# The second transform of a Fourier and MLP kernel: its fold moved behind the length-49 product, its token split moved to GpSimd

## The chip, the cores and the metric

One core of a Trainium2 chip runs the whole kernel in one launch. The metric is device time in microseconds (us), a median over runs; lower is better. The engines named below are TensorE (PE in the rows; PEld is its weight load), VectorE (DVE), ScalarE (ACT), GpSimd (POOL) and SyncE (SP), which issues every DMA of this kernel on one queue.

## What is computed

Three blocks follow each other on x of shape 2 x 3136 x 256 (batch, tokens, channels), all float32:

```python
# 1: a filter in the frequency domain along the tokens
X = np.fft.rfft(x, axis=1)
Yr = Xr @ w_r - Xi @ w_i + b_r ; Yi = Xr @ w_i + Xi @ w_r + b_i    # then a soft threshold of 0.01
y = np.fft.irfft(Y, n=3136, axis=1)
# 2: x + relu(layernorm(x) @ w_ch1) @ w_ch2, with a gain, 256 -> 1024 -> 256
# 3: a Fourier mix and another MLP of that size
mixed = np.real(np.fft.fft(np.fft.fft(x, axis=1), axis=2))
u = x + mixed
out = u + relu(layernorm(u) @ w_ch1) @ w_ch2
```

The change lies in the Fourier mix of block 3. A transform of length 3136 is done as 49 x 64: a length-49 product over the tokens, then a length-64 one, and a length-256 one over the channels. Since only the real part is wanted and the channel transform is symmetric, channel c and channel 256 - c are first combined: a sum in channels 1 to 127 and a difference in channels 129 to 255. Channels 0 and 128 have no partner. The combination ("the fold") is linear and acts on channels, the length-49 product acts on tokens, so either can come first.

## The kernel before

The tokens lie as 98 rows (49 x 2) of 32 x 256 = 8192 columns. Blocks 1 to 3 are staged so that TensorE always has work: the MLP of block 2 (`mlp1`, 13 chunks of up to 512 tokens) and that of block 3 (`mlp2`, 13 chunks) are the two long runs, and other work is hung on them by *hooks*: a hook `(k, "l1", f)` runs a function behind hidden block f (0 to 7) of chunk k, a hook `(k, "l2", i)` behind output tile i (0 to 3). The hooks set the priority; a planner, which estimates the time of every instruction, then writes each engine's order, and an engine works strictly in that order.

*A chunk.* `l1(f)` (L630 on) is six matmuls into one of three PSUM tiles "a" (lines L220 to L222 inside `mm3r`), ScalarE's ReLU (L641) and VectorE's remainder of it (L642), which frees the tile. `l2(i)` is eight pairs of matmuls (L658, L659) into PSUM "b" and two VectorE adds (L662, L663). `prep` normalizes the next chunk: statistics and small arithmetic on VectorE (L586 to L595) and, for the chunks marked `by_act` (`mlp1[8:12]` and `mlp2[1:5]`), the application on ScalarE in two passes of up to four instructions (L602 with a bias, L603 with a scale). The bias of L602 is the negated mean, a 128 x 4 tile `ng` made by VectorE at L599. `trans` then transposes on TensorE (L617, PSUM "c") and rounds the result into two parts, on ScalarE (L622 or L202) and VectorE (L623 or L210).

*The second transform, first half.* `Stage98` (L330 on) works in 16 steps per batch, each on 98 x 512 raw tokens. `load` brings them by DMA (L348) into the ring `r98` of four tiles, which `Front.load` (L706, the same ring) shares for what `mlp2` reads. `split` folds on GpSimd (L360 sum, L361 difference, L362 the two channels without a partner), rounds the result to its high part on ScalarE (`a_copy`, L202 in the rows, tile `s`) and subtracts that on GpSimd for the low part (L210, tile `s`). `step` multiplies with three matmuls (L220 to L222 into PSUM "c"), copies the 98 x 512 result on ScalarE (L202, tile `o`), lays two columns of channel 128, which come from a small product of their own (`middle`, `middle2`), over it on GpSimd (L405) and stores it (L406). `start` loads the middle column, loads two tiles and splits both at once. The ring `t98` of two tiles serves the transposes of block 1 and, in `mlp1`, the decoding of block 3's weights (lines L509 to L517).

*Where it runs.* Batch 0 starts behind output tile 0 of chunk 7 of `mlp1`, with its first step at `(8, "l1", 0)` and five steps to a chunk in chunks 8 to 10. Batch 1 starts behind output tile 0 of chunk 0 of `mlp2`, with its first step at `(0, "l2", 2)` and five steps to a chunk in chunks 1 to 3. These chunks of `mlp2` also run `Front.dmix` in their first layer, VectorE work of some seven instructions per pair (L205, L754 to L759) that ends in additions of two SBUF tiles (L756, L759).

Of the kernel before, what the change touches and what calls it, by code (L numbers as in the profile page):

```python
# [9 lines left out]
F32 = mybir.dt.float32  # L10
# [6 lines left out]
R98, S98, O98 = 4, 8, 4  # L17
# [18 lines left out]
PREP_BEHIND = (3, 2, 0)  # L36
APPLY_POOL = (0, 1)
APPLY_CHUNKS = 2
STAGE4_AT = ((8, "l1", 0),) + tuple((k, *at) for k in (8, 9, 10) for at in
                                    (("l1", 2), ("l1", 5), ("l2", 0), ("l2", 1), ("l2", 3)))  # L40
STAGE4_MLP2 = ((0, "l2", 2),) + tuple((k, *at) for k in (1, 2, 3) for at in
                                      (("l1", 2), ("l1", 5), ("l2", 0), ("l2", 1), ("l2", 3)))
STAGE4_FROM = ((7, "l2", 0), (0, "l2", 0))
WARM_UP = 10
TB = 2
I64 = mybir.dt.int64
AF = mybir.ActivationFunctionType
ALU = mybir.AluOpType
# [5 lines left out]
D = 256  # L54
NQ = 98
# [107 lines left out]
def fourier_moe_kernel(ctx, tc, x, w_r, w_i, b_r, b_i, g_ln, w11, w12, w21, w22,  # L163
                       t_ca, t_cam, t_cim, t_cb, t_ci, t_cb0, t_ci0, t_cd, t_ident, out):
    nc = tc.nc
# [3 lines left out]
    wk = ctx.enter_context(tc.tile_pool(name="wk", bufs=2))  # L169
# [5 lines left out]
    def psum(tag):  # L175
        return pp.tile([128, 512], F32, tag="ps" + tag, name="ps" + tag, bufs=ps_bufs[tag])
# [4 lines left out]
    def qslot(dt=F32R):  # L181
        return wk.tile([128, 1024], dt, tag="q", name="q", bufs=3)

    def wslot(dt=F32, n=128):
        return wk.tile([n, 512], dt, tag="w", name="w", bufs=WB)
# [15 lines left out]
    def a_copy(o, i, scale=1.0):  # L201
        nc.scalar.activation(out=o, in_=i, func=AF.Copy, scale=scale)  # L202
# [6 lines left out]
    def sub(eng, o, a, b):  # L209
        ins = eng.tensor_tensor(out=o, in0=a, in1=b, op=ALU.subtract)  # L210
        mark["pool" if eng is nc.gpsimd else "dve"] = getattr(ins, "ins", ins)
# [6 lines left out]
    def mm3r(ps, lh, ll, rh, rl, first, last):  # L218

        nc.tensor.matmul(out=ps, lhsT=lh, rhs=rh, start=first, stop=False)  # L220
        nc.tensor.matmul(out=ps, lhsT=ll, rhs=rh, start=False, stop=False)  # L221
        ins = nc.tensor.matmul(out=ps, lhsT=lh, rhs=rl, start=False, stop=last)  # L222
        mark["pe"] = getattr(ins, "ins", ins)
# [54 lines left out]
    class Forward:  # L278
# [7 lines left out]
        def load(self, k, cut=1):  # L286
            t = self.slot()[0:NQ]
            w = 1024 // cut
            for e in range(cut):
                ins = sp.dma_start(out=t[:, e * w:(e + 1) * w],  # L290
                                   in_=x[self.b, k][:, e * w:(e + 1) * w])
                mark["sp"] = getattr(ins, "ins", ins)
            self.raw[k] = t

        def step(self):
            g = self.g
            if g >= 16:
                return
            e = g % 2
            ps = psum(self.tag)  # L300
            nc.tensor.matmul(out=ps, lhsT=cam, rhs=self.raw[g // 2][:, e * 512:(e + 1) * 512], start=True, stop=True)  # L301
            ins = nc.vector.transpose(out=yg[self.b].rearrange("p k c -> p c k")[:, g * 16:(g + 1) * 16, :],
                                      in_=ps.rearrange("p (c j) -> p c j", j=32))
            mark["dve"] = getattr(ins, "ins", ins)
            self.g += 1
# [24 lines left out]
    def s98():  # L330
        return [next(s98_ring)[0:NQ] for _ in range(2)]


    class Stage98:
# [8 lines left out]
        def load(self):  # L343
            g = self.nl
            if g >= 16:
                return
            t = wk.tile([NQ, 512], F32, tag="r98", name="r98", bufs=R98)
            sp.dma_start(out=t, in_=self.src[:, g * 512:(g + 1) * 512])  # L348
            self.raw[g] = t
            self.nl += 1  # L350

        def split(self):
            g = self.ns
            if g >= 16:
                return
            t = self.raw.pop(g)
            f = wslot(n=NQ)
            v, w = (a.rearrange("q (j c) -> q j c", c=D) for a in (t, f))
            lo, hi = v[:, :, 1:128], v[:, :, 255:128:-1]
            nc.gpsimd.tensor_tensor(out=w[:, :, 1:128], in0=lo, in1=hi, op=ALU.add)  # L360
            nc.gpsimd.tensor_tensor(out=w[:, :, 129:256], in0=lo, in1=hi, op=ALU.subtract)  # L361
            nc.gpsimd.tensor_copy(w[:, :, 0:256:128], v[:, :, 0:256:128])  # L362
            h, l = s98()
            a_copy(h, f)
            sub(nc.gpsimd, l, f, h)
            self.hl[g] = (h, l)
            self.ns += 1

# [16 lines left out]
        def start(self):  # L385
            self.middle()
            self.load()
            self.load()
            self.split()
            self.split()  # L390

        def step(self):
            g = self.g
            if g >= 16:
                return
            if g == 0:
                self.middle2()
            self.load()
            self.split()
            h, l = self.hl.pop(g)  # L400
            ps = psum(self.tag)
            mm3r(ps[0:NQ, :], self.ch, self.cl, h, l, True, True)
            o = next(o98_ring)[0:NQ]
            a_copy(o, ps[0:NQ, :])
            nc.gpsimd.tensor_copy(o[:, 128:512:256], self.mid[:, 2 * g:2 * g + 2])  # L405
            sp.dma_start(out=self.dst[:, g * 512:(g + 1) * 512], in_=o)  # L406
            self.g += 1

# [151 lines left out]
    class Chunk:  # L560
# [19 lines left out]
        def prep_(self):  # L580
            nt, y = self.nt, self.y
            st = wk.tile([128, 4, 6], F32, tag="st", name="st")
            mv = wk.tile([128, 4, 2], F32, tag="mv", name="mv")
            sm = wk.tile([128, 4, 4], F32, tag="sm", name="sm")
            for i in range(nt):
                nc.vector.bn_stats(out=st[:, i, :], in_=y[:, i, :])  # L586
            for i in range(nt):
                nc.vector.bn_aggr(out=mv[:, i, :], in_=st[:, i, :])
            var = mv[:, 0:nt, 1]
            s0, q, t, r = (sm[:, k, 0:nt] for k in range(4))  # L590
            nc.scalar.activation(out=s0, in_=var, func=AF.Sqrt, bias=e4, scale=4.0)
            nc.vector.reciprocal(q, s0)
            nc.vector.scalar_tensor_tensor(out=t, in0=var, scalar=EPS, in1=q, op0=ALU.add, op1=ALU.mult)
            nc.vector.scalar_tensor_tensor(out=t, in0=s0, scalar=0.25, in1=t, op0=ALU.mult, op1=ALU.add)
            nc.vector.reciprocal(r, t)  # L595
            self.yn = qslot(F32).rearrange("p (i c) -> p i c", c=D)
            if self.by_act:
                ng = wk.tile([128, 4], F32, tag="ng", name="ng")
                nc.vector.tensor_scalar(out=ng[:, 0:nt], in0=mv[:, 0:nt, 0], scalar1=-1.0, scalar2=None, op0=ALU.mult)  # L599
            for i in range(nt):  # L600
                if self.by_act:
                    nc.scalar.activation(out=self.yn[:, i, :], in_=y[:, i, :], func=AF.Identity, bias=ng[:, i:i + 1])  # L602
                    nc.scalar.activation(out=self.yn[:, i, :], in_=self.yn[:, i, :], func=AF.Copy, scale=r[:, i:i + 1])  # L603
                    continue
                eng = nc.gpsimd if i in APPLY_POOL and self in mlp1[0:APPLY_CHUNKS] else nc.vector
                eng.tensor_scalar(out=self.yn[:, i, :], in0=y[:, i, :], scalar1=mv[:, i, 0:1],
                                  scalar2=r[:, i:i + 1], op0=ALU.subtract, op1=ALU.mult)
# [314 lines left out]
    mlp2 = chunks2(plan2, wv2)  # L922
# [6 lines left out]
    s4 = [Stage98(dX1[b], dA2[b], ca_h, ca_l, "c") for b in range(NB)]  # L929
    hooks = {}  # L930

    def after(k, i, f):

        def g():
            with tc.issue_after(mlp1[k].rest[i]):
                f()
        return g

    def behind_l1(chunks, k, f):

        def g():
            with tc.issue_after(chunks[k].last):
                f()
        return g

    def hook(k, part, i, f):
        hooks.setdefault((k, part, i), []).append(f)
# [5 lines left out]
    for k, i in STAGE3_MLP:  # L953
        hook(k, "l2", i, inv1)
    hook(*STAGE4_FROM[0], s4[0].start)
    for k, part, i in STAGE4_AT:
        hook(k, part, i, s4[0].step)
    run_mlp(mlp1, mlp2[0:2], hooks)
    hooks = {}
    hook(*STAGE4_FROM[1], s4[1].start)  # L960
    for at in STAGE4_MLP2:
        hook(*at, behind_l1(mlp2, at[0], s4[1].step) if at[1] == "l2" else s4[1].step)
    run_mlp(mlp2, [], hooks)
# [31 lines left out]
```

## Time and profile before

| | us |
|---|---|
| median of 3 runs (lowest, highest) | 831.86 (829.77, 834.3) |
| the profiled execution: its time | 831.31 |
| its span in the profile, first to last instruction | 829.5 |
| TensorE busy in it | 810.0 (98%) |
| VectorE / ScalarE / GpSimd busy | 533.4 / 313.5 / 139.9 |
| mean granted TensorE clock | 0.995 |

The span is the trace's own; the profiled execution's time beside it has some 1.8 us more around it. A busy engine is one with an instruction in flight; matmuls are pipelined, so their durations overlap. The clock is told as a share of 2.4 GHz.

### The profile page before, as it was taken

How to read it: one execution, taken by the hardware profiler on the slowest of the kernel's cores; microseconds unless marked ns; L12 is line 12 of the kernel's file. 1: busy time of each engine (PE TensorE's matmuls, PEld its weight loads, DVE VectorE, ACT ScalarE, POOL GpSimd, SP SyncE). 2: the span in 40 equal slices, each digit the busy share in tenths (PEclk: the TensorE clock that was granted, in tenths of full speed). 3: DMA queues.
4: the chain of work that ended last, by engine and by line, in shares of the span. 5: the costliest groups of instructions: out<-in, count | busy, mean ns of one | idle time of the engine just before them, and what ended most of it. 6: DMA issues, size and time to landing. Idle time of an engine off the chain costs nothing.

```text
span 829.5 us, 12209 instructions
## 1 busy us (share of the span) xinstructions
PE 810.0 (98%) x4456; PEld 676.6 (82%) x4456; DVE 533.4 (64%) x1244; ACT 313.5 (38%) x629; POOL 139.9 (17%) x202
## 2 busy tenths in 40 slices
PE   9999999999999999989999999999999999999996
PEld 3888977967878889868788887888888898888885
DVE  6579995475665688755547666637555666655653
ACT  1322356354343322364553125555642233322221
POOL 1222221320000000099210005345400000000000
PEclk9999999999999999999999999999999999999999
DMA  8642200721016211462233113344232121210001
GB/s 229 215 136 80 77 1 1 233 79 51 8 45 199 87 55 72 117 189 88 88 102 106 56 54 81 109 113 127 88 96 82 53 63 56 70 52 26 20 16 30
DMA packets 48175, 71.57 MB, mean 86 GB/s; under 512 B 11746, under 2 KB 32490, under 8 KB 47920
## 3 DMA queue, kind: packets, MB, share of 16 engines
q1 hardware_dynamic: 48116, 70.80, 27.9%
q8 instruction: 35, 0.57, 0.3%
q14 instruction: 24, 0.20, 0.1%
HBM read 45.09 MB, written 25.69 MB: 85 GB/s over the span
## 4 chain that ended last, share of the span: by engine, by line
PE 79%; DVE 9%; DMA 5%; ACT 2%; SPq 2%; issue 1%; POOL 1%; POOLq 0%; ACTq 0%
PE psb L658 20%; PE psa L220 11%; PE psb L659 10%; PE psa L221 10%; PE psa L222 10%; PE psb L461 3%; PE psc L320 3%; PE psc L722 3%; PE psc L617 2%; PE psa L429 1%; PE psc L481 1%; DMA h<-in_x_dram 1%; PE psc L301 1%; DVE h L642 1%; DMA r<-dX 1%
## 5 line engine op out<-in xcount | busy, mean ns | idle before, releaser
L641 ACT ACTIVATE h<-psa 128x512 fp32r<-128x512 f32 (+2 forms) x208 | 117.3, 573 | 247.5 <-PE psa L222 222.1
L642 DVE SCALAR_TENSOR_TENSOR h<-psa,h 128x512 fp32r<-128x512 f32 (+2 forms) x208 | 134.7, 654 | 93.0 <-ACT h L641 91.5
L658 PE MATMUL psb<-r2b,h 128*128 128x512 f32 x392 | 137.6, 399 | 0.0
L658 PE MATMUL psb<-r3a,h 128*128 128x512 f32 x392 | 137.3, 399 | 0.0
L659 PE MATMUL psb<-r3a,h 128*128 128x256 f32 x392 | 106.1, 282 | 0.0
L659 PE MATMUL psb<-r2b,h 128*128 128x256 f32 x392 | 105.5, 280 | 0.0
L220 PE MATMUL psa<-q,r3a 128*128 128x512 f32 (+2 forms) x208 | 84.1, 404 | 5.9 <-DVE h L642 3.1
L461 PE MATMUL psb<-wm,h 128*128 128x256 f32 (+1 forms) x600 | 88.8, 298 | 0.7 <-DVE w L467 0.7
L658 PEld LDWEIGHTS psb<-r3a,h 128*128 128x128 f32 x392 | 71.6, 188 | 15.6 <-PE psa L222 0.3
L658 PEld LDWEIGHTS psb<-r2b,h 128*128 128x128 f32 x392 | 71.9, 188 | 14.9
L220 PE MATMUL psa<-q,r2b 128*128 128x512 f32 (+2 forms) x208 | 82.3, 396 | 0.8 <-DVE h L642 0.4
L461 PEld LDWEIGHTS psb<-wm,h 128*128 128x128 f32 (+1 forms) x600 | 76.2, 189 | 8.5 <-issue 8.0
L662 DVE TENSOR_TENSOR o<-psb,yb 128x256 f32<-128x256 f32 x74 | 30.1, 421 | 80.1 <-PE psb L659 77.5
L221 PE MATMUL psa<-q,r3a 128*128 128x512 f32 (+2 forms) x208 | 79.9, 384 | 0.0
L222 PE MATMUL psa<-q,r3a 128*128 128x512 f32 (+2 forms) x208 | 78.6, 386 | 0.0
L221 PE MATMUL psa<-q,r2b 128*128 128x512 f32 (+2 forms) x208 | 78.4, 378 | 0.0
L222 PE MATMUL psa<-q,r2b 128*128 128x512 f32 (+2 forms) x208 | 78.1, 379 | 0.0
L659 PEld LDWEIGHTS psb<-r3a,h 128*128 128x128 f32 x392 | 73.7, 189 | 4.1 <-issue 1.0
L659 PEld LDWEIGHTS psb<-r2b,h 128*128 128x128 f32 x392 | 73.9, 189 | 3.0
L202 ACT ACTIVATE yg<-psc 98x512 f32<-98x512 f32 (+2 forms) x58 | 48.4, 860 | 55.0 <-PE psc L320 26.7
L210 POOL TENSOR_TENSOR h<-w 128x512 f32<-128x512 f32 (+1 forms) x26 | 34.5, 1328 | 109.1 <-DVE w L468 61.5
L220 PEld LDWEIGHTS psa<-q,r3a 128*128 128x128 f32 x208 | 39.7, 191 | 15.8 <-DVE h L642 5.0
(110 smaller groups left out, 1261.0 us busy)
## 6 DMA issues: line engine op xcount, KB each, us to landing
s<-in_moe_w_ch_dram SPq DMA_DIRECT2D x16, 512.0 KB
r<-dX SPq DMA_DIRECT2D x32, 196.0 KB
dA<-o SPq DMA_DIRECT2D x32, 196.0 KB
dY<-yg SPq DMA_DIRECT2D x12, 512.0 KB
r<-dA SPq DMA_DIRECT2D x48, 128.0 KB
dX<-o SPq DMA_DIRECT2D x11, 512.0 KB
yb<-dX SPq DMA_DIRECT2D x50, 64.0 KB
out_dram<-o SPq DMA_DIRECT2D x50, 64.0 KB
```

Source lines behind the costliest of these rows:

```text
L202: nc.scalar.activation(out=o, in_=i, func=AF.Copy, scale=scale)
L210: ins = eng.tensor_tensor(out=o, in0=a, in1=b, op=ALU.subtract)
L220: nc.tensor.matmul(out=ps, lhsT=lh, rhs=rh, start=first, stop=False)
L221: nc.tensor.matmul(out=ps, lhsT=ll, rhs=rh, start=False, stop=False)
L222: ins = nc.tensor.matmul(out=ps, lhsT=lh, rhs=rl, start=False, stop=last)
L320: nc.tensor.matmul(out=ps[0:NQ, :], lhsT=cim, rhs=t, start=True, stop=True)
L461: nc.tensor.matmul(out=ps[0:m, u * D:(u + 1) * D], lhsT=xv[:, o:o + m], rhs=wm_hl[wv][:, e, c, :], start=k == 0, stop=k == 11)
L641: nc.scalar.activation(out=h[:, 0:n], in_=ps[:, 0:n], func=AF.Relu)
L642: ins = nc.vector.scalar_tensor_tensor(out=l[:, 0:n], in0=ps[:, 0:n], scalar=0.0, in1=h[:, 0:n], op0=ALU.max, op1=ALU.subtract)
L658: nc.tensor.matmul(out=ps, lhsT=h[:, ts_], rhs=w2[:, f, :], start=f == 0, stop=False)
L659: nc.tensor.matmul(out=ps[:, 0:D], lhsT=l[:, ts_], rhs=w2[:, f, 0:D], start=False, stop=f == NF - 1)
L662: nc.vector.tensor_tensor(out=o, in0=ps[:, 0:D], in1=self.y[:, i, :], op=ALU.add)
```

## The change

It touches `Stage98`, one line of `prep_`, and the hooks.

- `load` takes its tile from the ring `t98` (two tiles) and no longer from `r98` (four, shared with `Front.load`, which now has it alone).
- `split` no longer folds. GpSimd copies the raw tile to its high part and subtracts for the low part. ScalarE has no part in it.
- `step` multiplies the raw parts, with the same three matmuls. Behind them ScalarE copies channels 0 to 127 (98 x 2 x 128) out of PSUM and lays the two columns of channel 128 beside them; VectorE then makes the difference and the sum, each 98 x 2 x 127, with one operand in PSUM and the other in the tile that ScalarE wrote. The store is as before.
- `start` loads only; the two first splits are a function of their own, `ahead`, hooked at `(8, "l1", 0)` and, for batch 1, at `(0, "l2", 1)`.
- Batch 0's steps begin at `(8, "l1", 4)`, six in chunk 8 and five in chunks 9 and 10; batch 1's first step moves from `(0, "l2", 2)` to `(0, "l2", 3)`.
- In `prep_` the negated mean `ng` is made by ScalarE.

```diff
-STAGE4_AT = ((8, "l1", 0),) + tuple((k, *at) for k in (8, 9, 10) for at in
-                                    (("l1", 2), ("l1", 5), ("l2", 0), ("l2", 1), ("l2", 3)))
-STAGE4_MLP2 = ((0, "l2", 2),) + tuple((k, *at) for k in (1, 2, 3) for at in
+STAGE4_AT = ((8, "l1", 4), (8, "l1", 7), (8, "l2", 0), (8, "l2", 1), (8, "l2", 2), (8, "l2", 3)) + tuple(
+    (k, *at) for k in (9, 10) for at in (("l1", 2), ("l1", 6), ("l2", 0), ("l2", 1), ("l2", 3)))
+STAGE4_AHEAD = ((8, "l1", 0), (0, "l2", 1))
+STAGE4_MLP2 = ((0, "l2", 3),) + tuple((k, *at) for k in (1, 2, 3) for at in
                                       (("l1", 2), ("l1", 5), ("l2", 0), ("l2", 1), ("l2", 3)))
...
-            t = wk.tile([NQ, 512], F32, tag="r98", name="r98", bufs=R98)
+            t = wk.tile([NQ, 512], F32, tag="t98", name="r98", bufs=TB)
...
             t = self.raw.pop(g)
-            f = wslot(n=NQ)
-            v, w = (a.rearrange("q (j c) -> q j c", c=D) for a in (t, f))
-            lo, hi = v[:, :, 1:128], v[:, :, 255:128:-1]
-            nc.gpsimd.tensor_tensor(out=w[:, :, 1:128], in0=lo, in1=hi, op=ALU.add)
-            nc.gpsimd.tensor_tensor(out=w[:, :, 129:256], in0=lo, in1=hi, op=ALU.subtract)
-            nc.gpsimd.tensor_copy(w[:, :, 0:256:128], v[:, :, 0:256:128])
             h, l = s98()
-            a_copy(h, f)
-            sub(nc.gpsimd, l, f, h)
+            nc.gpsimd.tensor_copy(h, t)
+            sub(nc.gpsimd, l, t, h)
...
             self.load()
             self.load()
+
+        def ahead(self):
             self.split()
             self.split()
...
-            a_copy(o, ps[0:NQ, :])
-            nc.gpsimd.tensor_copy(o[:, 128:512:256], self.mid[:, 2 * g:2 * g + 2])
+            v, w = (a.rearrange("q (j c) -> q j c", c=D) for a in (ps[0:NQ, :], o))
+            a_copy(w[:, :, 0:128], v[:, :, 0:128])
+            a_copy(w[:, :, 128], self.mid[:, 2 * g:2 * g + 2])
+            lo, hi = w[:, :, 1:128], v[:, :, 255:128:-1]
+            nc.vector.tensor_tensor(out=w[:, :, 129:256], in0=lo, in1=hi, op=ALU.subtract)
+            nc.vector.tensor_tensor(out=lo, in0=lo, in1=hi, op=ALU.add)
...
-                nc.vector.tensor_scalar(out=ng[:, 0:nt], in0=mv[:, 0:nt, 0], scalar1=-1.0, scalar2=None, op0=ALU.mult)
+                a_copy(ng[:, 0:nt], mv[:, 0:nt, 0], scale=-1.0)
...
+    hook(*STAGE4_AHEAD[0], after(8, 0, s4[0].ahead))
...
+    hook(*STAGE4_AHEAD[1], behind_l1(mlp2, 0, s4[1].ahead))
```

## Rows read from the trace of the kernel before

**Rows 1.** The page, busy time of an engine, share of span, instructions.

```profile
PE   810.0 (98%) x4456; PEld 676.6 (82%) x4456; DVE 533.4 (64%) x1244; ACT 313.5 (38%) x629; POOL 139.9 (17%) x202
```

**Rows 2.** The chain of work that ended last, shares of the span by engine.

```profile
PE 79%; DVE 9%; DMA 5%; ACT 2%; SPq 2%; issue 1%; POOL 1%; POOLq 0%; ACTq 0%
```

**Rows 3.** Stretches: length, busy us (count) of PE, PEld, DVE, ACT, POOL; clock; DMA.

```profile
350.00:360.00 10.00, 7.34 (x35) 5.96 (x34) 3.01 (x6) 3.77 (x7) 7.79 (x16) 0.83 0.83 214
...
370.00:380.00 10.00, 9.03 (x51) 7.38 (x50) 3.61 (x7) 7.09 (x16) 9.73 (x16) 1.00 0.43 135
...
390.00:400.00 10.00, 8.20 (x34) 6.26 (x33) 6.92 (x12) 6.87 (x16) 5.21 (x11) 0.86 0.23 76
...
420.00:430.00 10.00, 10.00 (x52) 8.13 (x51) 4.32 (x8) 5.67 (x11) 0.38 (x2) 1.00 0.38 130
...
510.00:520.00 10.00, 8.72 (x50) 6.87 (x49) 5.38 (x13) 5.38 (x14) 6.10 (x10) 1.00 0.41 101
...
560.00:570.00 10.00, 10.00 (x52) 8.27 (x51) 9.43 (x26) 5.60 (x14) 7.19 (x12) 1.00 0.39 125
```

**Rows 4.** Timeline, 348 to 357 us: start, length, engine, line; idle before, its releaser.

```profile
354.02 0.19 POOL L362 COPY w<-r 98x4 f32<-98x4 f32 x1
...
354.25 0.63 ACT L202 ACTIVATE s<-w 98x512 fp32r<-98x512 f32 x1 [5.79 <-POOL w L362]
...
354.78 0.67 ACT L622 ACTIVATE q<-psc,g_sb 128x512 fp32r<-128x512 f32 x1
...
355.50 0.50 PE L220 MATMUL psa<-q,r3a 128*128 128x512 f32 x1 [2.66 <-ACT q L622]
```

**Rows 5.** Chain of work that ended last, 366 to 400 us: start, length, what.

```profile
366.69 1.63 DVE ng L599
...
371.31 0.50 PE psa L220
...
388.74 4.36 DVE ng L599
...
396.09 0.50 PE psa L220
```

**Rows 6.** Two lines' own views: shortest, median, longest ns; first and last start.

```profile
L599 DVE TENSOR_SCALAR ng<-mv x8: 155/696/4354, 341.7 to 597.5; 128x4 f32<-128x4 f32 x8
...
L759 DVE TENSOR_TENSOR yb<-w,yb x24: 411/418/957, 475.6 to 795.3; 128x256 f32<-128x256 f32 x24
```

**Rows 7.** Chain of work that ended last, 480 to 530 us.

```profile
501.61 4.36 DMA r<-dX
...
512.72 1.61 ACT q L603 x4
...
514.37 0.77 PE psc L617 x5
```

**Rows 8.** Groups of instructions on GpSimd: count, busy us, mean ns, idle before them.

```profile
L210 POOL TENSOR_TENSOR s<-w,s 98x512 fp32r<-98x512 f32 x32 | 41.2, 1299 | 34.6 <-ACT s L202 34.5
...
L360 POOL TENSOR_TENSOR w<-r 98x254 f32<-98x254 f32 x32 | 24.3, 760 | 5.4 <-ACT s L202 2.8 <-DMA r<-dX 1.8 <-DVE w L205 0.8
...
L362 POOL COPY w<-r 98x4 f32<-98x4 f32 x32 | 7.1, 222 | 0.0
...
L405 POOL COPY o<-mid 98x2 f32<-98x2 f32 x32 | 6.2, 197 | 49.0 <-ACT o L202 49.0
```

**Rows 9.** Groups of instructions on ScalarE, and one on VectorE, as in rows 8.

```profile
L662 DVE TENSOR_TENSOR o<-psb,yb 128x256 f32<-128x256 f32 x74 | 30.1, 421 | 80.1 <-PE psb L659 77.5 <-DMA dA<-o 2.3
...
L202 ACT ACTIVATE s<-w 98x512 fp32r<-98x512 f32 x32 | 20.0, 626 | 14.8 <-POOL w L362 12.2 <-PE psc L221 2.6
...
L202 ACT ACTIVATE o<-psc 98x512 f32<-98x512 f32 x32 | 18.8, 595 | 17.8 <-PE psc L222 17.2
...
L202 ACT ACTIVATE w<-psc 128x256 f32<-128x256 f32 (+1 forms) x26 | 9.8, 379 | 33.3 <-PE psc L722 33.3
...
L202 ACT ACTIVATE mid<-psc 98x32 f32<-98x32 f32 x2 | 0.4, 182 | 0.0
```

## The prediction

> **What bounds the kernel now.** I read the page first: TensorE is busy for 810.0 of 829.5 us, the next engine, VectorE, for 533.4 [rows 1]. The chain of waits agrees: 79% of it is TensorE's own work [rows 2]. The change takes no matmul away and adds none, so it can only give back time in which TensorE stands still or runs slow, and it can lose as much as it makes TensorE wait.
>
> So the next view is the table of stretches, over the two spells in which the second transform's first half runs, from about 350 to 430 us and from 500 to 610 us. Most stretches there have TensorE busy for all of their 10 us. Four do not: it is idle for 10 - 7.34 = 2.66 us in the first, 0.97 in the second, 1.80 in the third and 1.28 in the fourth [rows 3]. In two of these the granted clock is below full as well, 0.83 and 0.86 on average [rows 3]: the clock has two levels, 1.2 and 2.4 GHz, so the half level held for twice the missing share, 3.4 and 2.8 us, and cost half of that in work at most, 1.7 and 1.4 us. In both, the engine stood idle for 1.8 us or more just before. Together 2.66 + 0.97 + 1.80 + 1.28 + 1.7 + 1.4 = 9.8 us. This is all that the change can win on what the trace shows.
>
> What ended each idle time is in the timeline and in the chain.
>
> - *At 355.5 us* TensorE had waited 2.66 us for ScalarE's L622, the rounded input of the next chunk. ScalarE had stood idle for 5.79 us in front of a high part of the split, whose fold on GpSimd (L362) was not ready; L622 was next in its queue [rows 4]. The DMA that `start` waits for stalls ScalarE, and through it TensorE.
> - *At 371.3 and 396.1 us* the chain runs through L599, the negation of 128 x 4 means on VectorE: 1.63 us and 4.36 us long [rows 5]. Its shortest is 155 ns [rows 6]. From there it goes over L602 on ScalarE, which needs `ng`, and the ReLU queued behind it, to the PSUM tile that TensorE wants.
> - *At 514.4 us* TensorE wants the normalized chunk that L603 on ScalarE has just finished [rows 7]; the chain goes back to the load of the second batch's first raw tile, 4.36 us [rows 7], again over a split on ScalarE.
>
> **The change part by part.**
>
> *The split leaves ScalarE.* A high part of 626 ns goes, 32 times; the copy of the product falls from 512 columns, 595 ns, to 256, which I price by the 379 ns of a 128 x 256 copy out of PSUM; the two columns of channel 128 come to it, priced by the smallest copy in the list, 182 ns [rows 9]. Per step 626 + 595 - 379 - 182 = 660 ns less, 21 us over 32 steps. Against that, eight negations come to ScalarE, between 0.18 and 0.38 us each [rows 9], at most 3 us. What counts is less the sum than the order: no ScalarE instruction waits for GpSimd in this stage any more. So the first idle time, 2.66 us and its slow clock of 1.7, goes, as does the 1.28 us at 514. I take all of it, 5.6 us; the lower bound is nothing, if something else holds L622.
>
> *The negation leaves VectorE.* It waits for nothing there that the trace names, and is long only beside GpSimd work: GpSimd is busy for 9.73 us of the stretch 370 to 380 [rows 3]. On ScalarE it stands in front of L602, where its result is needed, and one crossing between engines goes. I take both idle times and the slow clock, 0.97 + 1.80 + 1.4 = 4.2 us; the lower bound is nothing, if the delay moves along with it.
>
> The row leaves a question: 4.36 us is more than three of the longest GpSimd instruction of this stage, 1.30 us [rows 5, 8]. Either the negation was held behind several of them in a row, or about 3 us of its time has another cause, which could move along with it; that is the fourth rival. The Trainium skill, page "SBUF — State Buffer", section "Who interferes with whom", states that VectorE and GpSimd share a pair of ports, that a copy or one-input arithmetic on VectorE can claim it, and that whichever starts first keeps it for its whole instruction while the other waits. Taken at its word this rule explains one instruction of waiting, 1.30 us, and the sum by it would be 827.2 us; by the row, which I follow, it is 824.0.
>
> *GpSimd.* Per step the fold's two instructions of 760 ns (the difference, L361, repeats L360), the copy of 222 and the overlay of 197 go; the subtraction of 1,299 stays [rows 8]. A copy of 98 x 512 comes, which the trace does not show. It lies between the 222 ns of a copy of four columns and the 1,299 of a subtraction of the same width. The two-input instructions rise by 1299 - 760 = 539 ns over 512 - 254 = 258 columns, 2.1 ns a column; a copy reads one input in place of two, so I halve the slope and take 0.2 + 512 x 1.05 = 0.74 us, an estimate. Then a step costs 2.04 us of GpSimd in place of 3.24, 38 us less over 32 steps. GpSimd ends no chain by itself, so this is worth what it takes off its neighbours: L759, which reads two SBUF tiles on VectorE, takes 418 ns at its median and up to 957 [rows 6].
>
> *VectorE gets the fold.* Two instructions per step, 98 x 254 with one operand in PSUM, as near as can be to L662, 128 x 256 with one operand in PSUM, 421 ns [rows 9]: 0.84 us per step, 26.9 us over 32 steps. Where is the room? In the stretches of the table VectorE is busy for 3.01 to 9.43 us of 10 [rows 3]. Second layers have room. The first layers of `mlp2` chunks 1 to 3 have none: in 560 to 570 us VectorE is busy for 9.43 us [rows 3]. Two of a chunk's five steps hang there, so 3 x 2 x 0.84 = 5.0 us falls where VectorE is full. But TensorE is busy for all 10 us of that stretch [rows 3], so it has some slack against VectorE even there, and part of VectorE's load in it goes (the negation, and waiting beside GpSimd). Bounds: 0 if all is hidden, 26.9 us if each fold stands in TensorE's way. I take 2.0, less than half of the 5.0.
>
> *A new wait.* The fold waits on VectorE for ScalarE's copy. Behind it in VectorE's queue stand L642, which frees TensorE's PSUM tile, and L662, which frees the other. Before, GpSimd's overlay had this wait, and stood idle 49.0 us in all for it [rows 8], costing nothing, since only the store came behind. How much of it VectorE inherits depends on where the planner puts the fold; it would wait only with nothing else queued in front. The PSUM tile "c" is held longer by 0.84 us; there are three, and a step comes only every few microseconds (below).
>
> *The ring of two, and the DMA queue.* The DMAs are as many as before, 32 loads, 32 stores and two middle columns, on the one queue of SyncE. A load now waits until the split two steps earlier is over; behind it stand the chunk's loads and stores. A slot's turn is a landing, 4.36 us [rows 7], and a split, 2.04: 6.4 us, with two slots 3.2 us per step. The first batch's 16 steps fill GpSimd's spell from 350 to about 430, where it is down to 0.38 us in 10 [rows 3]: 5 us per step. So the ring holds, at no cost; GpSimd's copy at its upper bound gives 3.5 us per step, which still holds. The two moved starts (splits behind `(8, "l1", 0)`, first step four blocks later, six steps in chunk 8; one tile later in batch 1) add no instruction and pass their DMAs through the same queue in the same order; the last steps stay at chunk 10 and chunk 3, so what reads them is not later. The decoding of weights that shares `t98` lies ahead of batch 0's loads and behind its last ones: nothing.
>
> **The sum.** Against the profiled execution: 831.31 - 5.6 - 4.2 + 2.0 = 823.5 us. The median of the runs shown, 831.86, lies 0.55 above that execution, so I predict 824.0, with 820 to 828 for this case alone. A difference of 0.5%, 4.2 us, is about what a measurement of this kernel can tell from none: faster means below 827.7, slower above 836.0.
>
> **The rivals.**
>
> 1. *ScalarE's own burst is the limit* (chance 0.14). L602 and L603 are up to eight instructions in a row, L603's four alone 1.61 us [rows 7], and the ReLU stands behind them whether or not `ng` is late. Then only the first idle time goes, 2.66 + 1.7 = 4.4, less what the negations cost there, up to 3 us: 831.9 - 4.4 + 1.5 = 829. For it: the 0.97 and 1.80 us both end behind L602. Against it: there are eight negations [rows 6], so eight such bursts, and far fewer idle times.
> 2. *The fold on VectorE stands in TensorE's way* (0.13). VectorE waits for ScalarE's copy or is simply full, L642 comes late, and TensorE waits for the PSUM tile. It ends slower when the folds that cost TensorE their 0.84 us exceed (9.8 + 4.2) / 0.84 = 17 of 32; with 20 it is 831.9 - 9.8 + 16.8 = 839. For it: the 9.43 us [rows 3], and the inherited wait. Against it: 26 of 32 steps lie where VectorE has room.
> 3. *Splits or loads come late* (0.03): the matmul of a step waits for GpSimd. For that a copy would need 2 x 5 - 4.36 - 1.30 = 4.3 us, three times its upper bound, or the queue would have to stall; 838 if half of the 32 steps are late by 1 us beyond the gain kept: 831.9 - 9.8 + 16.
> 4. *Most of the long negation is not its neighbour's doing* (0.06): one GpSimd instruction held it, 1.30 us at most, and 3 us of the 4.36 stay in front of L602, with the idle 1.80 and the slow clock of 1.4 behind them. 824.0 + 3.2 = 827.2. For it: no wait is recorded inside the instruction. Against it: the shortest is 155 ns [rows 6], and the long ones lie in GpSimd's spells. The rule of the Trainium skill cited above (its page "SBUF — State Buffer") speaks for this rival.
>
> The forecast itself gets 0.64. Faster: 0.64 + 0.03 (half of the fourth, whose time lies on the bound) = 0.67; within 0.5%: 0.14 + 0.03 = 0.17; slower: 0.13 + 0.03 = 0.16. The range for 8 in 10 begins a little under the full gain with no price for the fold (831.9 - 9.8 = 822, and 2 us of neighbours' time that I did not count): 819.5; it reaches over the first and fourth rivals to 835, and leaves out the second and third.
>
> **What would show it.** Right: no idle time of TensorE over 1 us between 350 and 400 and near 514; the clock at full there; the negation on ScalarE under 0.4 us; the fold's instructions near 0.42 us each; GpSimd's work on the second transform near 65 us in place of 103; TensorE's busy share up. Wrong: waits of TensorE for L642 behind the fold in chunks 1 to 3 of `mlp2`, VectorE idle for ScalarE's copy, or a copy on GpSimd beyond 1.3 us. The prediction fails most easily if the planner, with other instructions to place, orders some engine worse somewhere else in the two spells.

## The result and the profile after

The changed kernel takes 840.08 us (median; 839.32 to 841.72), the kernel before 832.81 beside it. The ratio is 1.0126, interval 1.0088 to 1.0164: slower by about 1.3%, where the prediction had 824.0 and at most 835.0. Its profiled execution took 839.32 us, with a span of 837.5, 8.0 us more than before.

In its rows most lines bear a number one higher than before: ScalarE's copies are L203, the ReLU and its remainder L642 and L643, the matmuls of a product L221 to L223. The fold is L405 and L406, GpSimd's copy L359.

The page's busy times, then the chain's shares by engine, as in [rows 1] and [rows 2]:

```profile
PE 811.9 (97%) x4456; PEld 679.3 (81%) x4456; DVE 543.3 (65%) x1300; ACT 293.7 (35%) x637; POOL 104.2 (12%) x106
...
PE 82%; DMA 7%; DVE 7%; SPq 2%; ACT 1%; POOL 1%; issue 1%; ACTq 0%; POOLq 0%
```

ScalarE and GpSimd lost the work that they were to lose (20 and 36 us) and VectorE gained 10, net of what it was spared. TensorE's busy share fell, where the prediction had it rise. The DMA share of the chain is up from 5 to 7%, the first sign of what happened. The table of stretches, columns as in [rows 3]:

```profile
350.00:360.00 10.00, 9.16 (x46) 6.94 (x45) 5.06 (x12) 3.96 (x12) 4.81 (x7) 1.00 0.70 213
...
390.00:400.00 10.00, 10.00 (x55) 8.38 (x54) 6.24 (x12) 6.30 (x17) 6.05 (x6) 1.00 0.40 129
...
510.00:520.00 10.00, 9.59 (x53) 8.05 (x52) 4.29 (x9) 3.24 (x9) 2.46 (x4) 1.00 0.40 122
520.00:530.00 10.00, 5.43 (x21) 4.30 (x21) 5.12 (x18) 2.56 (x9) 1.72 (x2) 0.76 0.48 155
...
550.00:560.00 10.00, 6.10 (x35) 4.87 (x34) 1.57 (x4) 2.21 (x7) 2.54 (x4) 0.97 0.32 102
560.00:570.00 10.00, 10.00 (x43) 8.25 (x44) 8.67 (x28) 3.94 (x12) 1.25 (x1) 0.86 0.35 107
...
590.00:600.00 10.00, 5.68 (x16) 4.09 (x15) 5.23 (x15) 3.21 (x10) 0.00 (x0) 0.68 0.17 54
```

The first spell came out as forecast: 0.84 us of idle time is left between 350 and 400, most of it in pieces of 0.29 and 0.52 us, and the clock is full. The wait for L603 near 514 is gone too. The second spell has three new long idle times, 10 - 5.43 = 4.57, 3.90 and 4.32 us, one in each of chunks 1, 2 and 3 of `mlp2`, each with a slow clock in or behind it. The 0.41 us in 510 to 520 is no rest of the old 1.28: it ends at 516.74 us and is a small one of the same new kind, as TensorE's list of waits shows (sum, times, longest):

```profile
PE psa L221 <- DVE h L643: 13.2, 4, 4.6
```

Idle time in these stretches is 0.84 + 0.41 + 4.57 + 3.90 + 4.32 = 14.0 us in place of 6.7 [rows 3]. By the page TensorE is idle for 837.5 - 811.9 = 25.6 us in place of 829.5 - 810.0 = 19.5. That is 6.1 of the 8.0 us more of span; for the other 1.9 it is busy longer, which fits the slow clock in these rows.

What TensorE waits for, and what stands behind it, in the third of the long ones. First the chain, 584 to 600 us (start, length, what), then ScalarE's timeline from 583 and TensorE's from 594 us:

```profile
585.15 8.40 DMA dA<-o
...
593.57 0.20 ACT o L203
593.78 0.49 ACT h L642
...
594.29 0.70 DVE h L643
```

```profile
593.57 0.20 ACT L203 ACTIVATE o<-mid 98x2 f32<-98x2 f32 x1 [7.98 <-DMA dA<-o]
593.68 0.58 ACT L642 ACTIVATE h<-psa 128x512 fp32r<-128x512 f32 x1
...
595.04 0.79 PE L221 MATMUL psa<-q,r2b 128*128 128x512 f32 x1 [4.32 <-DVE h L643]
```

ScalarE stood still for 7.98 us in front of the write of two columns, `o<-mid`, because the tile that it writes was still being stored by a DMA issued 8.4 us earlier. Behind it in ScalarE's queue stood the ReLU that frees TensorE's PSUM tile. The write was in no hurry: the copy of the same step's product out of PSUM came at 610.74 us, 17 us later. Its one input, the middle columns, exists long before the product does, so the planner could put it early. Over the whole run (groups of instructions):

```profile
L203 ACT ACTIVATE o<-psc 98x256 f32<-98x256 f32 x32 | 12.0, 381 | 16.1 <-PE psc L223 15.9
L203 ACT ACTIVATE o<-mid 98x2 f32<-98x2 f32 x32 | 5.7, 201 | 63.2 <-DMA dA<-o 63.2
```

Thirty-two copies of 0.2 us held ScalarE for 63.2 us, 48.3 of them in the second spell (500 to 620 us).

### The profile page after: what moved, and what is told of

Read it like the earlier page. It is cut to its first block, busy times and chain, and to the rows that moved or that the text cites. A ratio compares the mean times of both kernels' runs of the same rounds, so it can differ in the third digit from the quotient of the medians.

```text
span 837.5 us, 12211 instructions
## 1 busy us (share of the span) xinstructions
PE 811.9 (97%) x4456; PEld 679.3 (81%) x4456; DVE 543.3 (65%) x1300; ACT 293.7 (35%) x637; POOL 104.2 (12%) x106
## 4 chain that ended last, share of the span: by engine, by line
PE 82%; DMA 7%; DVE 7%; SPq 2%; ACT 1%; POOL 1%; issue 1%; ACTq 0%; POOLq 0%
PE psb L659 21%; PE psa L221 11%; PE psb L660 10%; PE psa L222 10%; PE psa L223 10%; PE psb L462 4%; DMA dA<-o 3%; PE psc L321 3%; PE psc L618 2%; PE psc L723 2%; PE psc L302 2%; PE psa L430 2%; PE psc L482 1%; DMA h<-in_x_dram 1%; PE psa L748 1%; DVE t L319 1%
## 5 line engine op out<-in xcount | busy, mean ns | idle before, releaser
L642 ACT ACTIVATE h<-psa 128x512 fp32r<-128x512 f32 (+2 forms) x208 | 117.2, 573 | 229.9 <-PE psa L223 204.6
L643 DVE SCALAR_TENSOR_TENSOR h<-psa,h 128x512 fp32r<-128x512 f32 (+2 forms) x208 | 134.4, 654 | 87.2 <-ACT h L642 85.7
L221 PE MATMUL psa<-q,r2b 128*128 128x512 f32 (+2 forms) x208 | 85.2, 410 | 13.7 <-DVE h L643 13.2
L221 PE MATMUL psa<-q,r3a 128*128 128x512 f32 (+2 forms) x208 | 82.8, 398 | 0.4 <-ACT q L623 0.3
L222 PE MATMUL psa<-q,r2b 128*128 128x512 f32 (+2 forms) x208 | 80.6, 389 | 0.0
L223 PE MATMUL psa<-q,r2b 128*128 128x512 f32 (+2 forms) x208 | 80.3, 389 | 0.0
L222 PE MATMUL psa<-q,r3a 128*128 128x512 f32 (+2 forms) x208 | 78.7, 378 | 0.0
L223 PE MATMUL psa<-q,r3a 128*128 128x512 f32 (+2 forms) x208 | 78.1, 380 | 0.0
L203 ACT ACTIVATE yg<-psc 98x512 f32<-98x512 f32 (+2 forms) x58 | 48.5, 862 | 55.9 <-PE psc L482 27.0
L221 PEld LDWEIGHTS psa<-q,r2b 128*128 128x128 f32 x208 | 40.5, 195 | 23.2 <-DVE h L643 15.3
```

The costliest lines, as they stand in the source:

```text
L642: nc.scalar.activation(out=h[:, 0:n], in_=ps[:, 0:n], func=AF.Relu)
L643: ins = nc.vector.scalar_tensor_tensor(out=l[:, 0:n], in0=ps[:, 0:n], scalar=0.0, in1=h[:, 0:n], op0=ALU.max, op1=ALU.subtract)
```

## The experiments

Beside each run stands the kernel before, measured on the same chip; its median was 831.97 us beside the first four runs, 828.57 beside the next four and 831.88 beside the last four. So ratios are compared across these groups, and times only within one.

**The two columns behind the product.** One number of the changed kernel: ScalarE's copy writes channel 128 too, so the two columns can't be laid down before it. The instructions of TensorE, VectorE and GpSimd keep their order; only ScalarE's and SyncE's change.

```diff
-            a_copy(w[:, :, 0:128], v[:, :, 0:128])
+            a_copy(w[:, :, 0:129], v[:, :, 0:129])
```

> The changed kernel with one number different: ScalarE's copy out of PSUM writes channels 0 to 128 in place of 0 to 127, so the two columns of channel 128 have to be laid over it afterwards and can't be written before the product. First theory (the early write of these two columns waits on ScalarE for the landing of an old store, and the ReLU behind it comes late): the three idle times of TensorE of 4.6, 3.9 and 4.3 us in 500 to 610 us go with their slow clock, 19.7 us of lost time in all, so 820 to 824 us, with no wait of ScalarE for a store over 1 us. Rival (the fold's 26 us on VectorE, or the moved steps, keep TensorE waiting): nothing of this changes, 836 to 842 us.

Measured: 821.40 us, ratio 0.9878 (0.9845 to 0.9911). The two groups of ScalarE, and the stretches of the three idle times:

```profile
L203 ACT ACTIVATE o<-psc 98x258 f32<-98x258 f32 x32 | 12.2, 386 | 35.3 <-PE psc L223 34.6
L203 ACT ACTIVATE o<-mid 98x2 f32<-98x2 f32 x32 | 6.5, 205 | 0.7
```

```profile
520.00:530.00 10.00, 10.00 (x50) 8.20 (x49) 8.75 (x31) 5.32 (x16) 2.44 (x3) 1.00 0.53 162
...
550.00:560.00 10.00, 10.00 (x52) 8.37 (x51) 8.87 (x29) 5.20 (x15) 3.14 (x4) 1.00 0.39 122
...
590.00:600.00 10.00, 10.00 (x60) 8.58 (x59) 5.87 (x14) 3.39 (x10) 0.00 (x0) 1.00 0.33 81
```

All of the wait and all three idle times are gone, with VectorE at 8.87 of 10 us and the fold, the rings and the hooks as they were. From 490 to 630 us no wait of TensorE is left. This settles the cause, but for SyncE's order, which changed too; the run with the columns on GpSimd, below, keeps it. The version beats both kernels.

**A ring of three output tiles in place of four.**

```diff
-R98, S98, O98 = 4, 8, 4
+R98, S98, O98 = 4, 8, 3
```

> The changed kernel with three tiles in the ring of the second transform's outputs in place of four. First theory: the early write of the two columns now waits for the store three steps before, which is issued one step later, so ScalarE is held longer and oftener: TensorE idle by more than the present 13 us, 850 us or more. Rival (VectorE's fold or the moved steps): the ring has nothing to do with it, 838 to 842 us.

Measured: 843.06 us, ratio 1.0126 (1.0079 to 1.0173). A miss: the same ratio as the changed kernel. ScalarE's wait grew only a little:

```profile
L203 ACT ACTIVATE o<-mid 98x2 f32<-98x2 f32 x32 | 5.9, 202 | 69.1 <-DMA dA<-o 69.0
```

With a tile less, the write also stands later in ScalarE's order (the other engines keep theirs): it follows the same stores at about the same distance. So this run could not tell the ring's depth from the rest: the planner moved the write along with it. What stays the same in both is that a write which nobody needs yet stands close behind the issue of the store that it waits for.

**The negation alone**, in the kernel before (the line of `ng` from the change).

> The kernel before with one line of the change alone: the negated mean on ScalarE. The prediction's term: the idle times of 0.97 and 1.80 us and the slow clock behind the second go, 4.2 us less than the kernel before. Rival (the burst of L602 and L603 on ScalarE is the limit, or the delay moves along): less than 1 us of difference, and idle times remain near 371 and 396 us.

Measured: 830.25 us, ratio 0.9989 (0.9962 to 1.0016): no gain. The idle time near 396 us did go, and that near 371 shrank from 0.97 to 0.27 us; the first one grew. The stretches:

```profile
350.00:360.00 10.00, 6.54 (x35) 5.41 (x34) 3.20 (x6) 3.13 (x6) 6.04 (x13) 0.91 0.84 181
390.00:400.00 10.00, 10.00 (x48) 8.04 (x47) 7.45 (x20) 8.50 (x20) 7.41 (x14) 1.00 0.47 145
510.00:520.00 10.00, 8.78 (x44) 7.17 (x42) 3.05 (x8) 4.08 (x10) 4.42 (x8) 0.83 0.40 98
```

The start's wait of ScalarE costs 3.46 us here in place of 2.66, and a slow clock appears near 514. So the size of these is not a constant of the kernel: the edit moved the order of all engines' instructions, and with it the other waits.

**GpSimd makes the high part**, in the kernel before, the fold still in front.

```diff
-            a_copy(h, f)
+            nc.gpsimd.tensor_copy(h, f)
```

> The kernel before with one line different: the high part of the split is copied by GpSimd in place of ScalarE; the fold stays in front of the product. The prediction's term: ScalarE waits for GpSimd no more, the idle times of 2.66 us (with its slow clock) and of 1.28 us near 514 us go, some 5 us less than the kernel before. Rival: the 0.61 us more of GpSimd per step beside VectorE lengthens the negations on VectorE, and what was won is lost there, within 2 us of the kernel before.

Measured: 833.14 us, ratio 1.0020 (0.9998 to 1.0043): the rival. ScalarE's wait is gone, with the idle times that it caused, and a new idle time of TensorE of 5.7 us stands at 368. Its chain:

```profile
364.20 4.80 DVE ng L599
...
369.12 2.61 DVE sm L593
...
371.74 1.47 DVE sm L594
```

Three VectorE instructions on 128 x 4 elements take 8.9 us beside a GpSimd that works without a pause.

**Both lines together**, in the kernel before.

> The kernel before with two lines of the change together: the negated mean on ScalarE and the high part of the split copied by GpSimd; the fold stays on GpSimd in front of the product. Apart, neither gained, because what remained of the other took its place (the start's wait of ScalarE with the first, negations of 4.8 us on VectorE with the second). First theory: together they take both away, 9.8 us, so about 822 us, and the fold's move to VectorE is worth nothing by itself. Rival: with 3.9 us of GpSimd per step, VectorE's small two-input instructions beside it stay long (2.6 and 1.5 us in the run with the second line alone), and 826 to 831 us remain.

Measured: 832.80 us, ratio 1.0044 (1.0020 to 1.0068): the rival again. The long wait passed from the negation to the next small instruction. VectorE's and GpSimd's timelines, 363 to 372 us:

```profile
363.28 4.68 DVE L593 SCALAR_TENSOR_TENSOR sm<-mv,sm 128x4 f32<-128x4 f32 x1
368.00 2.67 DVE L594 SCALAR_TENSOR_TENSOR sm<-sm 128x4 f32<-128x4 f32 x1
```

```profile
363.47 0.61 POOL L364 CAST s<-w 98x512 fp32r<-98x512 f32 x1
364.05 2.53 POOL L210 TENSOR_TENSOR s<-w,s 98x512 fp32r<-98x512 f32 x2
366.54 0.72 POOL L360 TENSOR_TENSOR w<-r 98x254 f32<-98x254 f32 x1
367.23 0.72 POOL L361 TENSOR_TENSOR w<-r 98x254 f32<-98x254 f32 x1
367.89 0.18 POOL L362 COPY w<-r 98x4 f32<-98x4 f32 x1
```

So neither of the lines that the prediction put its gain on gives any of it while the fold stays on GpSimd.

**The negation back on VectorE**, in the version with the columns behind the product.

> The run with the columns of channel 128 laid after the product, with the negated mean back on VectorE. If the negation is long only beside a busy GpSimd, which now works 1.9 us per step in place of 3.2, it loses little: 821 to 823 us. If one long negation is enough, as at 389 us in the kernel before, up to 4.2 us more than that run: 825.6 us.

Measured: 821.40 us, ratio 0.9911 (0.9889 to 0.9933). The negation takes 437 ns on average on VectorE, 1.24 us at the longest, and the trace shows no wait of TensorE over 0.7 us in either spell. The time is that of the run with the columns behind the product on the other chip; the ratio is 0.3 to 0.5% above those of that run and of its repetition below. So the trace shows no cost, and the ratios leave up to some 4 us open.

**Twice the fold**, in the version with the columns behind the product (negation on ScalarE): the difference three times over, with the same result.

```diff
-            nc.vector.tensor_tensor(out=w[:, :, 129:256], in0=lo, in1=hi, op=ALU.subtract)
+            for _ in range(3):
+                nc.vector.tensor_tensor(out=w[:, :, 129:256], in0=lo, in1=hi, op=ALU.subtract)
```

> The run with the columns laid after the product, with the fold's difference computed three times in place of once, so that the fold's time on VectorE is doubled (26 us more). If the fold is hidden: within 1 us of that run, 821 to 823 us. The prediction's term of 2.0 us for the fold would make it about 2 to 5 us more, 823 to 826 us. If the fold stands in TensorE's way: up to 26 us more, with waits of TensorE for L643.

Measured: 823.71 us, ratio 0.9936 (0.9911 to 0.9961); 2.3 and 1.6 us above its two neighbours on that chip, the run before it and the one after it. The intervals of the ratios overlap, so this is a hint. Neither neighbour is the same version without the doubling: one has the negation on VectorE, the other lays the two columns on GpSimd. Against the ratios of that version itself, 0.9878 and 0.9860, it is 5 to 6 us. TensorE's waits for L644 (L643 elsewhere) in the second spell come to 0.6 us.

**GpSimd lays the two columns**, as early as the planner likes, in the changed kernel. TensorE, VectorE and SyncE keep the changed kernel's order, and ScalarE but for the 32 copies.

```diff
-            a_copy(w[:, :, 128], self.mid[:, 2 * g:2 * g + 2])
+            nc.gpsimd.tensor_copy(w[:, :, 128], self.mid[:, 2 * g:2 * g + 2])
```

> The changed kernel with the two columns of channel 128 laid by GpSimd in place of ScalarE, as early as the planner likes. First theory: the wait for the store moves to GpSimd, whose splits are some steps ahead, so TensorE hardly feels it: 820 to 826 us, with GpSimd idle for stores some 60 us in all. Rival (any engine held for 6 to 8 us makes the product late): TensorE waits for the split's tiles, 830 us or more.

Measured: 822.10 us, ratio 0.9915 (0.9886 to 0.9944). The wait is there as before, on another engine:

```profile
L403 POOL COPY o<-mid 98x2 f32<-98x2 f32 x32 | 5.9, 197 | 57.0 <-DMA dA<-o 56.9
```

GpSimd stands still for 56.9 us and TensorE hardly feels it, with 1.2 us of waiting for a split in all and none in the second spell: behind GpSimd's write stand splits of later steps, behind ScalarE's stood the ReLU. With the DMA order the same, this shows the cause a second time: it is the wait's place in ScalarE's queue.

**The version with the columns behind the product once more**, on the chip of the three runs that follow.

> The run with the columns of channel 128 laid after the product once more, on the chip of the three runs beside it, so that these are compared on one chip. Both theories: 819 to 824 us, 1.0 to 1.5% below the kernel before.

Measured: 820.38 us, ratio 0.9860 (0.9839 to 0.9880).

**Hooks and start of the kernel before**, in that version (its `STAGE4_AT` and `STAGE4_MLP2`, no `ahead`, both first splits in `start`).

> That run with the kernel before's hooks and start (both first splits at once, first step earlier). First theory (the hooks matter little once no engine that TensorE needs is held): within 2 us of it. Rival (the later steps give the first tiles time): TensorE waits for the first splits, near 353 and 505 us, and it is 3 us or more slower.

Measured: 821.41 us, ratio 0.9873 (0.9852 to 0.9894): 1.0 us more, within the intervals. The moved steps are worth nothing that can be told.

**The shared ring of four for the raw tiles**, in that version (`tag="r98"`, `bufs=R98`).

> That run with the raw tiles in the shared ring of four, as in the kernel before. The prediction gave the ring of its own no price and no gain: within 1.5 us of it. Rival (the ring shared with what block 3 reads delays the loads behind it on the one DMA queue): 3 us or more slower.

Measured: 822.06 us, ratio 0.9881 (0.9855 to 0.9907): 1.7 us more, again within the intervals. The ring is not what gains.

**Four times the fold**, in that version: the difference seven times over, with the same result.

> That run with the difference computed seven times, so that the fold takes four times its time on VectorE, some 79 us more. Each 26 us of it cost about 2 us in the run with twice the fold, if that difference was real: then 826 to 829 us. If the fold is hidden as long as VectorE has room: within 2 us, 820 to 824 us. If VectorE fills up in the first layers: waits of TensorE for L643 in each chunk and 835 us or more.

Measured: 835.15 us, ratio 1.0030 (1.0002 to 1.0058), 14.8 us above the run beside it. TensorE's waits for work of VectorE, two groups out of its list (sum, times, longest):

```profile
PE psb L660 <- DVE o L665: 4.8, 3, 3.4
PE psa L221 <- DVE h L644: 2.9, 4, 1.0
```

```profile
560.00:570.00 10.00, 10.00 (x54) 8.35 (x53) 9.97 (x28) 2.37 (x7) 4.46 (x5) 1.00 0.35 105
570.00:580.00 10.00, 6.65 (x30) 5.54 (x29) 8.13 (x25) 4.28 (x12) 1.88 (x2) 0.83 0.26 72
```

Whether the price is in proportion is open. With the 2 us that the first 26 us more cost beside their neighbours, the next 52 cost some 13; with the 5 to 6 us by the ratios, some 9 to 10. What the rows show is where the room ends: VectorE is busy for 9.97 us of 560 to 570 here, and TensorE idle for 3.35 us of the next stretch.

## Why the prediction was wrong

**The step that failed** is the one on ScalarE: "the two columns of channel 128 come to it, priced by the smallest copy in the list, 182 ns". The price was about right, 201 ns; the wait in front of it, 63.2 us in all, was put at nothing without being looked for. The part on new waits named the fold's wait for ScalarE's copy and the loads' wait for a split, and not that a write into the ring of outputs waits for an old store. In the kernel before, that wait stood in front of ScalarE's copy of the product, which comes so late that the store has always landed (no wait for a store stands in front of it there); GpSimd's overlay came behind that copy [rows 8]. The change cut the tie between the two, since the copy now leaves channel 128 alone. The sentence "no ScalarE instruction waits for GpSimd in this stage any more" held, and what was drawn from it, that ScalarE would not hold TensorE up, did not, because it now waited for a DMA. The run with 129 channels and the one with the columns on GpSimd show this cause: a ratio of 1.0126 with the wait on ScalarE, against 0.9878, 0.9860 and 0.9915 without, 17 to 22 us.

**The sum without that step** gave 823.5 us, 824.0 as a median, against 821.40 and 820.38 for the version without the wait. The size is close, since the idle times that it counted did go, but two of its terms are not had by the lines that they were put on. The 5.6 us for the split and the 4.2 for the negation were each put on one line. Alone, each line takes away the waits that it was to take away, or most of them, and others come in their place: no gain (0.9989 and 1.0020), and together a loss (1.0044). In the version without the wait the negation's own place makes no difference that the trace shows. What is left is the fold's leaving GpSimd, 1.7 us of its time a step, which the text gave no value but what it takes off its neighbours; that the sum comes out all the same is in part luck. By exclusion the gain lies there, since the hooks and the ring, each taken back, change nothing that can be told. No run moves the fold alone, with the high part still on ScalarE, or takes hooks and ring back together. The rows agree: with GpSimd's work thinned, VectorE's small instructions stay short, the negation 1.24 us at the longest in place of 4.35.

**Right.** The fold's instructions, forecast near 0.42 us: 413 and 415 ns. GpSimd's copy, forecast 0.74 within 0.22 to 1.30: 614 ns. GpSimd's work on the second transform, forecast 65 us: 41.0 + 19.4 = 60.4. The ring of two and the moved steps at no price: within 1.7 us. The idle times of the first spell gone, in the changed kernel as forecast. VectorE did wait for ScalarE's copy, a sign that the prediction named for being wrong, but for 11.3 us in all (8.9 without the wait on ScalarE), and this cost TensorE nothing that a trace shows.

**The fold's price**, 2.0 us, was too high as far as the trace tells: in the version without the wait TensorE's matmuls wait for L643 once, for 0.2 us. Doubling the fold cost 2 to 6 us.

**A slip in the reading.** Of the stretches in the two spells six are short of 10 us and not four: 530 to 540 and 590 to 600 have 0.18 us of idle time each. The version without the wait has TensorE busy for all of these too.

**The rivals.** None of the four was it. The first would have left the idle times near 371 and 396 us, and they are gone; the third needs waits for splits, and there is one of 0.52 us. The second came nearest, with TensorE held by L643 in chunks 1 to 3 of `mlp2`, but VectorE was idle there (1.57 us busy in 550 to 560), waiting for ScalarE. The fourth fell: the runs with GpSimd busy throughout show 4.80, 4.68 and 2.67 us on three different small instructions of VectorE, always over several GpSimd instructions in a row.

## What to carry to other kernels

An instruction with early inputs can be placed early, and then waits for whatever it lacks in front of everything behind it on its engine. When a small write is cut loose from the large one that it used to follow, ask what else it waits for, above all the buffer it writes, and which engine's queue can afford that wait; tying it to the large one again, here by one column, costs nothing. And price an edit on a crowded engine by the whole change: two lines that each took away a wait were worth nothing as long as the work beside which both waits arose had not moved.

## What the hardware showed beside this

A VectorE instruction on 128 x 4 elements, 0.16 us long elsewhere, took 4.68 us beside seven GpSimd instructions without a pause, and the next one 2.67. The Trainium skill, page "SBUF — State Buffer", section "Who interferes with whom", states that a VectorE instruction with two SBUF inputs contends with GpSimd's reads, which these rows bear out. The Trainium skill, same page, section "SBUF: two separate sides", states that the one that starts first keeps the shared ports for its whole instruction; here the wait went on over the starts of five later ones.

The waits end where one GpSimd instruction gives way to the next, yet not at the first such place. The two above end at 367.96 and 370.67 us, 0.07 us behind the start of GpSimd's copy of four columns (367.89 and 370.60), and went over the starts of five and three instructions before. What decides this, no run shows.

A store of 98 x 512 elements landed between 2.3 and 8.5 us after its issue, as far as ScalarE's waits tell: one issued at 595.83 us released the write at 598.09. Two late ones in the second spell (chain, other stretches than above):

```profile
519.93 6.24 DMA dA<-o
```

```profile
549.88 8.53 DMA dA<-o
```

That the loads and stores of the chunks, on the same queue, delayed them is likely and was not tried.
